# Splitting the first seven weight pieces on Pool, with a mask word spread over their shift

## The chip, the cores and the metric

The kernel runs on one core of one Trainium2 chip. Its five engines work side by side, each in the order of its own queue: TensorE (PE; its weight loads are listed apart as PEld), VectorE (DVE), ScalarE (ACT), GpSimd (Pool) and SyncE (SP), which here only issues DMAs. The metric is the device time of one execution in microseconds. Before the change it is 633.34 us, the median of three runs (632.31 to 634.42).

## The reference, cut to what matters

Attention with a local window and a few global keys, over 4 batches, 8 heads, 768 positions and a head size of 64, and then a feed-forward network (FFN) on the 3072 tokens that come out:

```
scores = q @ k^T / 8 + bias            # bias = -slope[head] * distance
scores = where(global | local, scores, -1e9)
x = softmax(scores) @ v                # 3072 tokens x 512
h = x @ w_in                           # 512 x 2048, float64
out = maximum(0.01 * h, h) @ w_out     # 2048 x 512, float64, result float32
```

`w_in` and `w_out` are float64 numbers. The kernel reads them as pairs of 32-bit words and turns every number into a sum of two rounded numbers (type fp32r), a high and a low part, so that three matmuls of fp32r stand for one exact product.

## The kernel before, in words

**The work and its stages.** The attention is cut into 48 units of one block of 128 queries and four heads. For a unit, TensorE makes the scores (L218), DVE adds the bias and finds the smallest value in one pass (L232), ACT takes exponentials with their sums (L245), DVE makes reciprocals (L266, L267), a diagonal matrix of them is made (`dg`, L284, by Pool in the first eight units and by DVE after), TensorE transposes and scales with it (L314), ACT copies the result (`pt`, L329), TensorE multiplies it by `v` (L360), and the product is split into a high part by ACT (`xh`, L387) and a low part by DVE (`xl`, L390).

The FFN takes the tokens in chunks: the first two of 384, the rest of 256. The weights lie in 32 pieces of 128 x 512 float64 (16 of `w_in`, 16 of `w_out`), and each is converted once. Seven of them (`LEAD_CONV`) are converted in the lead, which is the stage ahead of the FFN; the other 25 are converted between the FFN's first tiles.

**The lead.** The loop at the end of `fast_path` calls `lead_event(t)` for t = 0 to 7. Event t holds the scores of unit t, the product with `v` of unit t-2, the transposes of unit t-1, and from t = 1 on the conversion of piece t-1. The order of the instructions on every engine is written out by hand and pinned (`pin`, `keep_in_program_order`).

**A conversion** (`split_float64`) has six steps. `scale`: ACT turns the upper word into a float32 of the right exponent (L939). `shift`: DVE shifts its bits by three and masks them (L942), then brings the sign in from the upper word (L944). `low`: DVE brings in the upper bits of the lower word (L948). `high`: ACT rounds the number to its high part (L952). `rest`: DVE subtracts the high part from the number (L955). The work tile `w` of these steps has two buffers.

The first three steps of piece p stand in event p+1. Its last two, `high` and `rest`, are put on a list (`due`) and are issued in the event behind: `ends[0]()` at the event's beginning, `ends[1]()` behind the exponentials. So in event t the instructions of DVE stand in this order: four L232 of unit t, `rest` of piece t-2, both instructions of `shift` of piece t-1, the two small operations of `sums`, `low` of piece t-1, and L390 of unit t-2, which ends the event (in event 7, the last, `xl` stands behind the L232). Those of ACT: `high` of piece t-2, `scale` of piece t-1, four exponentials, the copy `pt` of unit t-1, `xh` of unit t-2. Pool has only `dg` of unit t, and, between units 0 and 1, eight small scalings of the bias table (L1010). The last two steps of the seventh piece (p = 6) stand in the FFN's first tile (j = 0).

**The loads.** SP issues the loads of q, k, v and of the weight pieces (L121), the latter three pieces ahead of their conversion, into four staging buffers. Two converted pieces of `w_in` are also written out to DRAM by SP early on (L886, `wd<-ring`), from a ring of two buffers that streams weights later.

Of the kernel before, what the change touches and what calls it, by code (L numbers as in the profile page):

```python
# [10 lines left out]
F32 = mybir.dt.float32  # L11
F32R = mybir.dt.float32r
BF16 = mybir.dt.bfloat16
I32 = mybir.dt.int32
I64 = mybir.dt.int64
AF = mybir.ActivationFunctionType
ALU = mybir.AluOpType
# [18 lines left out]
LEAD_CONV = 7  # L36
# [12 lines left out]
def copy_exact(eng, dst, src):  # L49
    return eng.tensor_scalar(out=dst, in0=src, scalar1=1.0, scalar2=1.0, op0=ALU.mult, op1=ALU.mult)  # L50
# [3 lines left out]
def fast_path(ctx, tc, qp, kp, vp, wi, wo, nvec, convert, nmall, out, B, H, S):  # L54
    nc = tc.nc
# [19 lines left out]
    raw = ctx.enter_context(tc.tile_pool(name="raw", bufs=2))  # L75
# [14 lines left out]
    stage = early.enter_context(tc.tile_pool(name="stage", bufs=STAGES, side="right"))  # L90
# [7 lines left out]
    small = const.tile([P, 32], F32, name="one")  # L98
    one, ones, fl = small[:, :1], small[:, 1:2], small[:, 4:8]
    flag = small[:1, 8:9].bitcast(I32)  # L100
    nc.vector.memset(one, 0.0)
    pinned_exp = nc.scalar.activation(out=one, in_=one, func=AF.Exp)
    tc.keep_in_program_order(pinned_exp)
# [3 lines left out]
    eye = const.tile([P, HALF], F32, name="eye")  # L107
    tc.keep_in_program_order(nc.vector.tensor_tensor(out=eye, in0=ident[:, :HALF], in1=ident[:, HALF:], op=ALU.add))
    convert()
    nbw = const.tile([P, H, KW], BF16, name="nbw")  # L110
    nb0 = const.tile([P, H, KW - HALF], BF16, name="nb0")

# [2 lines left out]
    staged = {}  # L115

    def load_piece(p):
        if p < len(pieces):
            m, f = pieces[p]
            t = stage.tile([P, NK * P], I64, tag="stage", name="wst", bufs=STAGES)  # L120
            pin(nc.sync.dma_start(out=t, in_=(wi, wo)[m][f].rearrange("p a b -> p (a b)")))  # L121
            staged[p] = t
# [10 lines left out]
    def conversion(p):  # L133

        m, f = pieces[p]
        to = wout[:, f] if m else win[f]
        dh, dl = to[:, 0], to[:, 1]
        if p:
            load_piece(p + STAGES - 2)
        scale, shift, low, *parts = split_float64(tc, pin, stage, staged.pop(p), dh, dl)  # L140
        due.extend(parts)
        return scale, shift, low

# [2 lines left out]
    LEAD = NU * CHUNKS[0]  # L146
# [234 lines left out]
    def parts(u, av):  # L381
        del units[u]
        av = av[:, :, 2 * KW:]
        xh, xl = slab(u)

        def high():
            pin(nc.scalar.copy(out=xh, in_=av))  # L387

        def low():
            pin(nc.vector.tensor_tensor(out=xl, in0=av, in1=xh.bitcast(F32), op=ALU.subtract))  # L390
        return high, low
# [12 lines left out]
    def lead_event(t, conv=(), between=lambda: None):  # L404

        av = (ps_lead if t % 2 else ps_x).tile([P, 2, 512], F32, tag="ps_av", name="ps_sc")
        high, low = [lambda: None] * 2
        last = t == LEAD + 1
        scores(t, av)
        if t > 1:  # L410
            ov = ps_lead.tile([P, 2, 512], F32, tag="ps_ov", name="ps_ov")
            attn_v(t - 2, ov)
            high, low = parts(t - 2, ov)
        if t:
            transposes(t - 1)
        if t:
            load_qk(t + 2)
        load_v(t)
        if t < 2:
            load_piece(t + 1)  # L420
        ends = due[:] or [lambda: None] * 2
        due.clear()
        ends[0]()
        if last:
            high()
        scale, shift, low_bits = conversion(conv[0]) if conv else [lambda: None] * 3
        scale()
        biased(t, av)
        if last:
            low()  # L430
        exps(t)
        between()
        ends[1]()
        shift()
        sums(t)
        low_bits()
        if t:
            keep_pt(t - 1)
        if not last:
            high()  # L440
            low()
# [315 lines left out]
    load_qk(2)  # L757
    warm(5)
    tabs = kept_rows.tile([P, 2, KW], BF16, name="tabs")
    tables = build_bias(tc, ffn, nb0, nvec, tabs, H)  # L760
    with tc.tile_pool(name="ps_l", bufs=1, space=bass.MemoryType.PSUM) as ps_lead:
        for t in range(LEAD + 2):
            lead_event(t, [t - LEAD - 2 + LEAD_CONV] if t >= LEAD + 2 - LEAD_CONV else (), *([] if t else [tables]))
            if t == 0:
                scale_bias(tc, tabs[:, 1], nbw, H, 1)
    ps_h = ctx.enter_context(tc.tile_pool(name="ps_h", bufs=1, space=bass.MemoryType.PSUM))
# [2 lines left out]
    for j in range(len(order)):  # L769
# [5 lines left out]
        scale, shift, low_bits = conversion(todo[0]) if todo else [lambda: None] * 3  # L775
# [5 lines left out]
        if events and j < LEFT:  # L781
            t = events[0]
# [11 lines left out]
            high, low = parts(t - 2, av)  # L794
# [78 lines left out]
        if j in twice:  # L873
            ends = due[:]
            due.clear()
            scale, shift, low_bits = conversion(todo[1])
# [47 lines left out]
    return last_pairs()  # L924


def split_float64(tc, pin, pool, raw, dh, dl):

    nc = tc.nc
    w2 = raw.bitcast(I32).rearrange("p (n two) -> p n two", two=2)
    lo, hi = w2[:, :, 0], w2[:, :, 1]
    w = pool.tile([P, lo.shape[1]], F32, tag="work", name="w32", bufs=2)
    wb = w.bitcast(I32)
    w3 = w.rearrange("p (a b) -> p a b", a=dh.shape[1]) if len(dh.shape) == 3 else w

    def scale():
        pin(nc.scalar.activation(out=w, in_=hi.bitcast(F32), func=AF.Copy, scale=2.0 ** -112))  # L939

    def shift():
        pin(nc.vector.tensor_scalar(out=wb, in0=wb, scalar1=3, scalar2=0x7FFFFFF8,  # L942
                                    op0=ALU.logical_shift_left, op1=ALU.bitwise_and))
        pin(nc.vector.scalar_tensor_tensor(out=wb, in0=hi, scalar=-0x80000000, in1=wb,  # L944
                                           op0=ALU.bitwise_and, op1=ALU.bitwise_or))

    def low():
        pin(nc.vector.scalar_tensor_tensor(out=wb, in0=lo, scalar=29, in1=wb,  # L948
                                           op0=ALU.logical_shift_right, op1=ALU.bitwise_or))

    def high():
        pin(nc.scalar.copy(out=dh, in_=w3))  # L952

    def rest():
        pin(nc.vector.tensor_tensor(out=dl, in0=w3, in1=dh.bitcast(F32), op=ALU.subtract))  # L955

    return scale, shift, low, high, rest


def build_bias(tc, work, nb0, nvec, tabs, H):  # L960

    nc = tc.nc
    pin = tc.keep_in_program_order
    loc = work.tile([P, 2 * P], F32, tag="gh", name="loc")
    far = work.tile([P, 2 * P], F32, tag="gl", name="far")
    col = work.tile([P, HALF], F32, tag="gh", name="col")
    n8 = work.tile([P, 1], F32, tag="gl", name="n8")
    first, tab = tabs[:, 0], tabs[:, 1]  # L970
    ng, nl = nvec[:, 0:1], nvec[:, 1:2]
    lo, hi = slice(0, HALF), slice(HALF, P)


    nc.gpsimd.iota(loc, pattern=[[8, 2 * P]], base=-8 * P, channel_multiplier=-8, allow_small_or_imprecise_dtypes=True)
    nc.gpsimd.affine_select(out=loc[:, P:], in_=loc[:, P:], pattern=[[-1, P]], compare_op=ALU.is_ge, fill=-BIG, base=0,
                            channel_multiplier=1)
    nc.gpsimd.iota(col, pattern=[[1, HALF]], base=0, channel_multiplier=0, allow_small_or_imprecise_dtypes=True)
    nc.gpsimd.memset(first[lo, HALF:P], -BIG)
    pin(nc.vector.tensor_scalar(out=n8, in0=nl, scalar1=-8.0, scalar2=None, op0=ALU.mult))  # L980
    pin(nc.vector.tensor_scalar(out=col, in0=col, scalar1=ng, scalar2=-BIG, op0=ALU.is_ge, op1=ALU.mult))
    pin(nc.vector.tensor_scalar(out=far, in0=loc, scalar1=n8, scalar2=-BIG, op0=ALU.is_le, op1=ALU.mult))
    pin(nc.vector.tensor_tensor(out=loc, in0=loc, in1=far, op=ALU.add))

    for part, x in ((lo, HALF), (hi, 0)):
        pin(nc.vector.scalar_tensor_tensor(out=first[part, HALF + x:P + x], in0=col[part], scalar=n8[part],
                                           in1=loc[part, P:P + HALF], op0=ALU.add, op1=ALU.max))
    pin(nc.vector.tensor_copy(out=first[hi, P:], in_=loc[hi, P + HALF:]))
    for h in range(H):
        pin(nc_scale(nc, nc.vector if h < H // NU else nc.scalar, nb0, first[:, HALF:], h, H, 1))  # L990

    def tables():
        for part, x, y in ((lo, HALF, G), (hi, 0, P - G)):
            pin(nc.vector.tensor_scalar(out=tab[part, x:x + G], in0=col[part, :G], scalar1=n8[part], scalar2=None, op0=ALU.add))
        pin(nc.scalar.copy(out=tab[lo, :HALF], in_=loc[lo, P - WIN:P - G]))
        pin(nc.scalar.copy(out=tab[lo, HALF + G:], in_=loc[lo, P - G:P + HALF]))
        pin(nc.scalar.copy(out=tab[hi, G:], in_=loc[hi, P - G:]))
    return tables
# [248 lines left out]
```

## Time and profile before

| What | Value |
|---|---|
| Time, median of three runs | 633.34 us |
| The profiled execution's own time | 633.62 us |
| Its span, from the first to the last instruction | 631.8 us |
| Mean clock granted to TensorE | 0.997 |
| Busy in 0 to 40 us: PE, DVE, ACT, Pool | 26.72, 33.59, 32.28, 11.71 us |
| Busy in 40 to 60 us: PE, DVE, ACT, Pool | 18.99, 18.31, 16.22, 3.53 us |
| Busy in 60 to 100 us: PE, DVE, ACT, Pool | 40.00, 33.91, 25.24, 3.30 us |
| DMA: share of time busy, 0 to 40 us | 0.84 |

How to read the profile. A row of the timeline gives the start and the duration in us, the engine, the line of the kernel, the operation, the tile written and the tiles read with their shapes, how many instructions the row stands for, and in brackets how long the engine stood idle before it and what ended that. Durations of two neighbours on one engine may overlap by some hundredths, because an instruction starts while the one ahead of it drains; so the time that an instruction takes on its engine is read from start to start. A row of a single line gives the count, the shortest, the median and the longest duration in ns, the first and the last start, and the shapes. The slices of the page cut the span into 40 equal parts; each digit is the busy share in tenths. The spans of Pool are rougher than those of the other engines.

### The profile page before, as it was taken

Reading aid. Unit: us, or ns where it says so; the run is one execution under the profiler, and the core shown is the slowest. Engines: PE = TensorE matmul, PEld = TensorE weight load, DVE = VectorE, ACT = ScalarE, POOL = GpSimd, SP = SyncE. Lnnn points to the kernel's source line nnn. Section 1 sums busy time; section 2 is a strip of 40 time slices with the busy share of each in tenths; the row PEclk is TensorE's granted clock in tenths of the full one; section 3 lists DMA queues with packets and bytes.
Section 4 is the critical chain, followed back from the end, with each engine's and each line's share of the span. In section 5 each row is a group of like instructions: output and inputs, shape, how many; then the busy total and the mean of one; then the engine's idle time right before and its main releaser. Section 6 shows DMA issues by size and latency. Waiting matters only on the chain.

```text
span 631.8 us, 16777 instructions
## 1 busy us (share of the span) xinstructions
PE 609.2 (96%) x6546; PEld 561.9 (89%) x6546; DVE 457.7 (72%) x1308; ACT 345.3 (55%) x901; POOL 68.6 (11%) x118
## 2 busy tenths in 40 slices
PE   5789999999999999999999999999999999999994
PEld 4578899988888888899999999999999999999994
DVE  7988879995566996966986765765765766754653
ACT  6987755554435556546556555545655655522321
POOL 4212200000101001011012101101101100110000
PEclk9999999999999999999999999999999999999998
DMA  7886645633547755765765865855865864633321
GB/s 262 312 307 196 198 146 188 200 109 122 159 140 243 243 186 183 227 206 192 227 219 175 264 239 162 262 175 172 247 229 182 258 211 143 217 102 101 134 68 38
DMA packets 63336, 120.72 MB, mean 191 GB/s; under 512 B 8976, under 2 KB 28432, under 8 KB 63248
## 3 DMA queue, kind: packets, MB, share of 16 engines
q1 hardware_dynamic: 52880, 82.34, 40.5%
q10 hardware_dynamic: 10368, 37.23, 18.0%
q8 instruction: 53, 0.87, 0.6%
q14 instruction: 35, 0.29, 0.2%
HBM read 96.21 MB, written 23.33 MB: 189 GB/s over the span
## 4 chain that ended last, share of the span: by engine, by line
PE 85%; DVE 6%; DMA 4%; ACT 3%; issue 1%; SPq 0%; DVEq 0%; ACTq 0%
PE ps_m L612 21%; PE ps_p L556 16%; PE ps_h L556 15%; PE ps_h L472 9%; PE ps_q L612 7%; PE ps_av L360 5%; PE ps_av L218 3%; PE ps_o L1180 3%; PE ps_o L1179 3%; PE ps_o L1181 3%; ACT pr L245 2%; DMA ring<-wd 1%; DVE pr L232 1%; DMA via<-pr 1%; DVE w L948 1%
## 5 line engine op out<-in xcount | busy, mean ns | idle before, releaser
L578 ACT CAST gh<-t 128x896 fp32r<-128x896 f32 (+1 forms) x73 | 62.2, 853 | 100.0 <-DVE t L572 57.5
L581 DVE TENSOR_TENSOR gl<-t,gh 128x896 fp32r<-128x896 f32 (+1 forms) x73 | 71.1, 974 | 47.9 <-ACT gh L578 47.9
L245 ACT ACTIVATE pr<-pr,nmall 128x192 f32<-128x192 f32 (+1 forms) x192 | 83.3, 435 | 25.4 <-DVE nmall L232 25.4
L612 PE MATMUL ps_m<-wout,gh 128*128 128x256 f32 (+1 forms) x396 | 85.9, 299 | 0.0
L569 DVE SCALAR_TENSOR_TENSOR t<-t 128x512 f32<-128x512 f32 x72 | 49.6, 689 | 33.0 <-ACT t L567 31.8
L50 POOL TENSOR_SCALAR xh<-x 128x256 fp32r<-128x256 f32 x36 | 22.7, 631 | 433.1 <-ACT x L366 352.6
L472 PE MATMUL ps_h<-xh,win 128*128 128x384 f32 x224 | 62.7, 341 | 0.2 <-DVE xl L390 0.2
L612 PEld LDWEIGHTS ps_m<-wout,gh 128*128 128x128 f32 x396 | 61.4, 188 | 1.6
L612 PE MATMUL ps_m<-wout,gl 128*128 128x256 f32 (+1 forms) x198 | 59.2, 299 | 0.0
L556 PE MATMUL ps_p<-xh,win 128*128 128x256 f32 x288 | 58.3, 287 | 0.0
L556 PE MATMUL ps_h<-xh,win 128*128 128x256 f32 x288 | 56.8, 282 | 0.0
L556 PE MATMUL ps_h<-xh,ring 128*128 128x256 f32 x288 | 55.6, 278 | 0.0
L556 PE MATMUL ps_p<-xh,ring 128*128 128x256 f32 x288 | 55.3, 277 | 0.4 <-DMA ring<-wd 0.4
L572 DVE TENSOR_TENSOR t<-t 128x128 f32<-128x128 f32 x216 | 53.1, 284 | 2.8
L556 PEld LDWEIGHTS ps_p<-xh,win 128*128 128x128 f32 x288 | 46.3, 188 | 6.0 <-issue 5.0
L556 PEld LDWEIGHTS ps_h<-xh,win 128*128 128x128 f32 x288 | 46.5, 188 | 2.4 <-issue 2.2
L232 DVE CUSTOM_DVE_ANT_0 pr<-ps_av,nbw 128x192 f32<-128x192 f32 x136 | 40.3, 351 | 11.1 <-ACT x L366 9.3
L612 PE MATMUL ps_m<-h,gh 128*128 128x256 f32 (+1 forms) x162 | 46.9, 290 | 0.0
L556 PEld LDWEIGHTS ps_p<-xh,ring 128*128 128x128 f32 x288 | 46.2, 188 | 0.6 <-DMA ring<-wd 0.6
L556 PEld LDWEIGHTS ps_h<-xh,ring 128*128 128x128 f32 x288 | 46.4, 189 | 0.0
L612 PE MATMUL ps_m<-h,gl 128*128 128x256 f32 x162 | 45.0, 278 | 0.0
L612 PE MATMUL ps_m<-l,gh 128*128 128x256 f32 x162 | 45.0, 278 | 0.0
(154 smaller groups left out, 1567.1 us busy)
## 6 DMA issues: line engine op xcount, KB each, us to landing
ring<-wd ACTq DMA_DIRECT2D x70, 512.0 KB, 3.6
via<-pr SPq DMA_DIRECT2D x30, 384.0 KB, 3.2
pt_d<-via SPq DMA_DIRECT2D x120, 96.0 KB, 3.2
vr<-in_vp_dram SPq DMA_DIRECT2D x40, 256.0 KB, 3.4
kr<-in_kp_dram SPq DMA_DIRECT2D x39, 256.0 KB, 4.0
wst<-in_wi_dram SPq DMA_DIRECT2D x16, 512.0 KB, 4.5
wst<-in_wo_dram SPq DMA_DIRECT2D x16, 512.0 KB, 4.5
qs<-in_qp_dram SPq DMA_DIRECT2D x24, 256.0 KB, 4.5
```

The lines of the kernel that those rows point to most:

```text
L50: return eng.tensor_scalar(out=dst, in0=src, scalar1=1.0, scalar2=1.0, op0=ALU.mult, op1=ALU.mult)
L218: tc.keep_in_program_order(nc.tensor.matmul(own(u, av[qf, j, a * KW:(a + 1) * KW]), lhsT=q[rows, a, qf], rhs=keys(rows, a, f), start=True, ...
L232: pin(nc.vector.tensor_tensor_reduce(out=head(u, pr, a, j), in0=own(u, ps[:, j, a * KW:(a + 1) * KW]), in1=nb, scale=-0.125, scalar=3.0e38 ...
L245: pin(nc.scalar.activation(out=p, in_=p, func=AF.Exp, scale=-1.0, bias=nm[:, 2 * a + j:2 * a + j + 1], accum_out=sm[:, 2 * a + j:2 * a + j ...
L360: tc.keep_in_program_order(nc.tensor.matmul(av[out, a, cols], lhsT=v[rows, t, j, :], rhs=near(rows, j, t, fs), start=(n == 0), stop=(n == ...
L472: tc.keep_in_program_order(nc.tensor.matmul(ps, lhsT=win[f][:, y, k], rhs=xt[c][x][:, k, :ct], start=(k + i == 0), stop=(k == NK - 1 and i ...
L556: tc.keep_in_program_order(nc.tensor.matmul(o, lhsT=w[:, y, k], rhs=x[:, k, :], start=(k + i == 0), stop=(k == NK - 1 and i == 2)))
L569: pin(nc.vector.scalar_tensor_tensor(out=g, in0=g, scalar=0.01, in1=g, op0=ALU.mult, op1=ALU.max))
L572: pin(nc.vector.tensor_tensor(out=t[:, o], in0=t[:, x], in1=t[:, y], op=op))
L578: pin(nc.scalar.copy(out=gh[:, i - a0:j - a0], in_=t[:, i:j]))
L581: pin(nc.vector.tensor_tensor(out=gl[:, i - a0:j - a0], in0=t[:, i:j], in1=gh[:, i - a0:j - a0].bitcast(F32), op=ALU.subtract))
L612: tc.keep_in_program_order(nc.tensor.matmul(to, lhsT=x[:, a], rhs=y, start=first and n == 0, stop=last and n == 2))
```

## The change

For the seven pieces of the lead (`p < LEAD_CONV`), `high` and `rest` go to Pool: the rounding as a multiplication by one (`copy_exact`, an existing helper), the subtraction as before. Their places in the order of the program stay. Of the shift, the shift with its mask becomes an operation on two tensors, by DVE as before: the mask is no longer a constant of the instruction but a word in a column of `small`, spread over the 512 elements. This word is made in two steps: a memset of the column, and in event 0, behind the exponentials, an operation on that column. The other 25 pieces are converted as before.

```
+    mask = small[:, 10:11].bitcast(I32)
...
+    make_mask = lambda: pin(nc.vector.tensor_scalar(out=mask, in0=mask, scalar1=0, scalar2=0x7FFFFFF8,
+                                                    op0=ALU.bitwise_and, op1=ALU.bitwise_or))
...
-        scale, shift, low, *parts = split_float64(tc, pin, stage, staged.pop(p), dh, dl)
+        scale, shift, low, *parts = split_float64(tc, pin, stage, staged.pop(p), dh, dl, mask if p < LEAD_CONV else None)
...
+    nc.vector.memset(small[:, 10:11], 0.0)
...
-            lead_event(t, [t - LEAD - 2 + LEAD_CONV] if t >= LEAD + 2 - LEAD_CONV else (), *([] if t else [tables]))
+            lead_event(t, [t - LEAD - 2 + LEAD_CONV] if t >= LEAD + 2 - LEAD_CONV else (), *([] if t else [lambda: (tables(), make_mask())]))
...
     def shift():
-        pin(nc.vector.tensor_scalar(out=wb, in0=wb, scalar1=3, scalar2=0x7FFFFFF8,
-                                    op0=ALU.logical_shift_left, op1=ALU.bitwise_and))
+        if mask is None:
+            pin(nc.vector.tensor_scalar(out=wb, in0=wb, scalar1=3, scalar2=0x7FFFFFF8,
+                                        op0=ALU.logical_shift_left, op1=ALU.bitwise_and))
+        else:
+            pin(nc.vector.scalar_tensor_tensor(out=wb, in0=wb, scalar=3, in1=mask.to_broadcast(list(wb.shape)),
+                                               op0=ALU.logical_shift_left, op1=ALU.bitwise_and))
         pin(nc.vector.scalar_tensor_tensor(out=wb, in0=hi, scalar=-0x80000000, in1=wb,
                                            op0=ALU.bitwise_and, op1=ALU.bitwise_or))
...
     def high():
-        pin(nc.scalar.copy(out=dh, in_=w3))
+        pin(copy_exact(nc.gpsimd, dh, w3) if mask is not None else nc.scalar.copy(out=dh, in_=w3))

     def rest():
-        pin(nc.vector.tensor_tensor(out=dl, in0=w3, in1=dh.bitcast(F32), op=ALU.subtract))
+        eng = nc.gpsimd if mask is not None else nc.vector
+        pin(eng.tensor_tensor(out=dl, in0=w3, in1=dh.bitcast(F32), op=ALU.subtract))
```

More of the change, by code (lines that the diff above doesn't have):

```diff
@@ L924, in fast_path, with split_float64 @@
     return last_pairs()
-def split_float64(tc, pin, pool, raw, dh, dl):
+def split_float64(tc, pin, pool, raw, dh, dl, mask=None):
     nc = tc.nc
```

## The prediction, made before the change was run

> **What bounds the kernel now.** I read the page first (busy shares, the span in 40 slices), then the timeline of the first 45 us, since the seven pieces are converted there, then single lines of Pool and windows in which Pool and DVE work at once.
>
> ```profile
> span 631.8 us, 16777 instructions
> ...
> PE 609.2 (96%) x6546; PEld 561.9 (89%) x6546; DVE 457.7 (72%) x1308; ACT 345.3 (55%) x901; POOL 68.6 (11%) x118
> ...
> PE   5789999999999999999999999999999999999994
> ...
> DVE  7988879995566996966986765765765766754653
> ACT  6987755554435556546556555545655655522321
> ```
>
> Over the span TensorE is the bound. Only in the first slices (15.8 us each) is it not, and there DVE and ACT are nearly full. Behind them TensorE has next to no idle time in which a delay of the lead could vanish: what the lead gains or loses, the end gains or loses. One event of the lead, in the timeline (start, duration, engine, line):
>
> ```profile
> 16.77 0.42 DVE L390 TENSOR_TENSOR xl<-ps_ov,xh 128x256 fp32r<-128x256 f32 x1
> ...
> 24.89 0.42 DVE L390 TENSOR_TENSOR xl<-ps_ov,xh 128x256 fp32r<-128x256 f32 x1
> ...
> 25.22 0.34 DVE L232 CUSTOM_DVE_ANT_0 pr<-ps_sc,nbw 128x192 f32<-128x192 f32 x1
> ...
> 26.33 0.68 DVE L955 TENSOR_TENSOR wout<-w,wout 128x512 fp32r<-128x512 f32 x1
> ...
> 26.93 0.42 DVE L942 TENSOR_SCALAR w<-w 128x512 int32<-128x512 int32 x1
> ...
> 27.39 0.69 DVE L944 SCALAR_TENSOR_TENSOR w<-wst,w 128x512 int32<-128x512 int32 x1
> ...
> 28.07 0.17 DVE L266 TENSOR_SCALAR rs<-sm 128x4 f32<-128x4 f32 x1
> 28.27 0.18 DVE L267 RECIPROCAL rs<-rs 128x4 f32<-128x4 f32 x1
> 28.37 0.66 DVE L948 SCALAR_TENSOR_TENSOR w<-wst,w 128x512 int32<-128x512 int32 x1
> ...
> 28.62 0.88 POOL L284 TENSOR_TENSOR dg<-eye,rs 128x256 f32<-128x256 f32 x1 [3.18 <-DVE rs L267]
> 28.95 0.42 DVE L390 TENSOR_TENSOR xl<-ps_ov,xh 128x256 fp32r<-128x256 f32 x1
> 29.06 0.62 ACT L952 CAST win<-w 128x512 fp32r<-128x512 f32 x1
> ...
> 29.59 0.69 ACT L939 ACTIVATE w<-wst 128x512 f32<-128x512 f32 x1
> ...
> 33.01 0.42 DVE L390 TENSOR_TENSOR xl<-ps_ov,xh 128x256 fp32r<-128x256 f32 x1
> ```
>
> From one L390 to the next is 4.06 us, and DVE goes through it without a gap. By starts: L390 0.33, four L232 1.11, the subtraction L955 0.60, the shift L942 0.46, the or L944 0.68, sums 0.20 and 0.10, low bits L948 0.58. Four such periods (events 3 to 6) lie between 16.77 and 33.01. Pool does one thing in a period, the dg product.
>
> **What leaves.** ACT loses L952, 0.53 to its next start (29.06 to 29.59), DVE loses L955, 0.60. Both stand in the full part of the lead, so this is the gain on offer.
>
> **The shift.** As an operation on two tensors it has L944's form, 0.69 for the same 512 elements, instead of 0.42. The or needs its result and starts 0.04 behind its end today (26.93 + 0.42 = 27.35, start 27.39), so 0.46 becomes 0.73. The word of the mask costs a memset of one column and one 128x1 operation, both in the first event or ahead of it, where DVE stands idle for ACT:
>
> ```profile
> 8.73 0.17 DVE L266 TENSOR_SCALAR rs<-sm 128x4 f32<-128x4 f32 x1 [0.80 <-ACT pr L245]
> ```
>
> The 0.80 hides an operation of 0.17; uncovered it would cost that, once.
>
> **Event 2**, the first with a subtraction, supplies the or's price without a wait, and a first look at what Pool does to DVE:
>
> ```profile
> 13.76 0.61 POOL L284 TENSOR_TENSOR dg<-eye,rs 128x256 f32<-128x256 f32 x1
> ...
> 13.88 1.05 DVE L955 TENSOR_TENSOR win<-w,win 128x512 fp32r<-128x512 f32 x1
> ...
> 14.85 0.41 DVE L942 TENSOR_SCALAR w<-w 128x512 int32<-128x512 int32 x1
> ...
> 15.30 0.69 DVE L944 SCALAR_TENSOR_TENSOR w<-wst,w 128x512 int32<-128x512 int32 x1
> ...
> 15.91 0.16 DVE L266 TENSOR_SCALAR rs<-sm 128x4 f32<-128x4 f32 x1
> ...
> 16.20 0.66 DVE L948 SCALAR_TENSOR_TENSOR w<-wst,w 128x512 int32<-128x512 int32 x1
> ```
>
> Here the or takes 0.61 (15.30 to 15.91). Undisturbed, the period would thus be 4.06 - 0.60 + 0.27 - 0.07 = 3.66: 0.40 saved.
>
> **What Pool takes.** No Pool row has 512 elements. The nearest (min/median/max ns, then two rows of the timeline):
>
> ```profile
> L1010 POOL TENSOR_SCALAR nbw<-tabs x16: 350/351/779, 9.8 to 59.3; 128x192 bf16<-128x192 bf16 x16
> L1010 POOL TENSOR_SCALAR nb<-tabs x8: 297/324/787, 64.0 to 71.7; 128x128 bf16<-128x128 bf16 x8
> ```
>
> ```profile
> 152.66 0.40 POOL L50 TENSOR_SCALAR xh<-x 128x256 fp32r<-128x256 f32 x1 [80.53 <-ACT pr L245]
> 153.15 0.74 POOL L397 TENSOR_TENSOR xl<-x,xh 128x256 fp32r<-128x256 f32 x1
> ```
>
> With one input 297, 350 and about 400 ns at 128, 192 and 256 elements are 0.83 ns an element on 0.19 us, so the high part is 0.19 + 0.43 = 0.62 (bounds 0.40, one row of half its size, and 0.80, two). The subtraction has two inputs: 0.74 at 256, of which 0.19 fixed, gives 0.19 + 2 x 0.55 = 1.29 at 512. Its bounds are 0.95 (second half at the one-input slope) and 1.48 (twice 0.74); I take 1.29, as its fixed part is read from three sizes. A dependent Pool instruction starts 0.09 behind (153.06 to 153.15). [...]
>
> **Pool and DVE hold each other up.** Beside dg (13.76 to 14.37) L955 took 1.05 instead of 0.68: it ended at 14.93 as if begun at 14.25, 0.12 ahead of dg's end. The reverse: dg at 28.62 took 0.88 instead of 0.61, as if begun at 28.89, when L948 was nearly through. Later, with the same operation as the one that moves:
>
> ```profile
> 224.23 0.79 POOL L397 TENSOR_TENSOR xl<-x,xh 128x256 fp32r<-128x256 f32 x1
> ...
> 224.34 0.96 DVE L592 TENSOR_TENSOR wk<-wout 128x256 f32<-128x256 f32 x1
> ```
>
> ```profile
> L592 DVE TENSOR_TENSOR wk<-wk,wout 128x256 f32<-128x256 f32 x42 | 17.3, 424 | 0.2
> ```
>
> 0.96 instead of 0.42: as if begun at 224.88, 0.14 ahead of Pool's end at 225.02. So a DVE instruction with two inputs in SBUF waits for a Pool instruction that was there first, less 0.13. L390 and L232, with one input in PSUM, don't: L390 at 28.95 has its 0.42 beside dg. [...]
>
> Now the steady event, counted from L390's start. Dg ends at 0.55 (29.50 against 28.95). The high part, queued behind it, 0.55 to 1.17; subtraction 1.26 to 2.55. DVE is through L232 at 1.44 and wants the shift, with two inputs in SBUF: it is let in at 2.42, a wait of 0.98. Behind it queue the or, the sums (and so dg) and the low bits, the whole rest of the event. Period 3.66 + 0.98 = 4.64, that is 0.58 more than 4.06; over four periods +2.3.
>
> Event 2: the shift wants to start at 13.88, gets in behind dg at 14.25; the high part, waiting since 14.37, comes next (14.78 to 15.40) and holds the or to 15.27; the subtraction gets in behind the or, about 15.80 to 17.09; the low bits start at 16.96 instead of 16.20: +0.75.
>
> **Events 7 and after.** The last subtractions fall here:
>
> ```profile
> 37.24 0.17 DVE L266 TENSOR_SCALAR rs<-sm 128x4 f32<-128x4 f32 x1 [0.31 <-ACT pr L245]
> ...
> 42.14 0.42 DVE L390 TENSOR_TENSOR xl<-ps_av,xh 128x256 fp32r<-128x256 f32 x1
> ...
> 42.66 0.90 PE L360 MATMUL ps_av<-pt,vr 64*64 64x128 f32 x32 [0.26 <-ACT pr L245]
> ```
>
> In event 7 the sums wait for ACT's exponentials, so a held shift costs nothing. In the first FFN tile the chain goes L390, then L360, which overwrites the bank that L390 reads; without the seventh L955 ahead of it, DVE comes sooner, and up to TensorE's wait of 0.26 is won. I book all of it: TensorE is full behind it, so no more can be.
>
> **Queues.** SP sends ring weights to DRAM when their subtraction is done, with loads behind it:
>
> ```profile
> 22.98 0.33 SPq L886 DMA_DIRECT2D wd<-ring  x1
> ...
> 23.84 0.74 SPq L121 DMA_DIRECT2D wst<-in_wo_dram  x1
> ```
>
> ```profile
> wst<-in_wo_dram SPq DMA_DIRECT2D x4, 512.0 KB, 5.3
> ```
>
> That piece lands at 29.14, its scale L939 starts at 29.59: 0.45 to spare. Pool ends this subtraction 2.55 into its event, where DVE ended it at 22.96, 2.1 after its own event began, so the load comes 0.4 later within the event; but the events are longer, and it stays in time. ACT, 0.53 shorter, is not late. The converted pieces themselves are wanted microseconds later.
>
> **The sum.** 2.3 + 0.75 - 0.26 = +2.8. The profiled execution took 633.62 us (span 631.8), 0.3 above the median of 633.34; I add to the median: 636.1. With the subtraction at 0.95 or 1.48, five events change by 0.34 or 0.19 each: +1.1 or +3.7. A measurement of this kernel tells about 0.3% (1.9 us) from no change.
>
> **Rivals.** (1) Faster: the shift by two tensors isn't held, because a spread word is read differently from a full tensor, which no row shows. Then events 3 to 6 give 4 x 0.40, event 2 gives 0.68 (no L955 with its 0.37 of waiting), the first tile 0.26: -2.5, 630.8. Against it: L944, L948 and L955 are of this kind, and are held or hold. (2) The same, but the loads become late: with periods of 3.66 event 6 wants its piece near 27.0, and SP can't issue it before the ring's subtraction is done (19.75 + 2.55, near 22.4) and 0.9 more, landing at 28.6: 1.5 of the gain go, -1.0, 632.3, no measurable change. (3) Slower still: Pool comes a little later (from a high part beyond 0.8, say), so that the shift slips in ahead of the subtraction, or ahead of the high part when that is not begun by 1.44; then the or is held for the high part too, 0.48 more in each of four periods: +4.7, 638.0. It decides at 1.44 in the event.
>
> **How the numbers follow.** Holding as worked out 0.72, of which 0.12 within 0.3% (a subtraction nearer 0.95); rival 1 0.12; rival 2 0.10; rival 3 0.06. Hence slower 0.66, same 0.22, faster 0.12. The range runs from 632.8 to 638.1: it takes in both bounds of the subtraction (634.4, 637.0), a share of rival 2 and rival 3, and leaves rival 1 out.
>
> **What would show it.** Right: Pool rows of about 0.62 and 1.29 per piece; L390 to L390 near 4.6; the shift's row near 1.7, its own 0.69 plus the wait; the L390 that is at 33.01 now near 36. Wrong: shift rows of 0.69 beside a running Pool subtraction (rival 1), L939 waiting for a load (rival 2), long rows of both shift and or in every event (rival 3), or a period of 4.6 with an unchanged end, if TensorE could make up the lead's delay.

## The result, and the profile after

The changed kernel takes 635.58 us (median of 7 runs, 635.24 to 640.07); the kernel before, on the same chip between them, 632.51 us (7 runs, 632.02 to 634.42). The ratio is 1.0056, with a 95% interval of 1.0039 to 1.0073: slower, by about 3.1 us. The profiled execution took 635.27 us.

From the page of the changed kernel, the lines that answer to those of before (the last is the clock granted to TensorE, in tenths):

```profile
span 633.5 us, 16779 instructions
...
PE 611.1 (96%) x6546; PEld 564.3 (89%) x6546; DVE 459.7 (73%) x1303; ACT 341.8 (54%) x894; POOL 83.7 (13%) x132
...
PE   5689999999999999999999999999999999999996
...
DVE  7989879996565997875987765765765765744654
ACT  6778755555344655555555654654664564522321
...
PEclk9789999999999999999999999999999999999999
```

ACT is 3.5 us less busy, Pool 15.1 us more, and DVE, which lost seven subtractions, is 2.0 us more busy. A row's duration includes the time in which the instruction is held (the shift's rows below: 0.69 and 1.60), so DVE's gain sits inside longer rows. One event of the lead shows where. Timeline of the changed kernel; line numbers grow by 3 up to L393 and by 4 to 9 behind it (the shift is L950, the or L952, the low bits L956; Pool's high part is L50 and its subtraction L964):

```profile
26.25 0.90 POOL L287 TENSOR_TENSOR dg<-eye,rs 128x256 f32<-128x256 f32 x1 [1.71 <-DVE rs L270]
26.60 0.41 DVE L393 TENSOR_TENSOR xl<-ps_ov,xh 128x256 fp32r<-128x256 f32 x1
...
27.13 0.61 POOL L50 TENSOR_SCALAR wout<-w 128x512 fp32r<-128x512 f32 x1
...
27.82 1.27 POOL L964 TENSOR_TENSOR wout<-w,wout 128x512 fp32r<-128x512 f32 x1
...
28.04 1.60 DVE L950 SCALAR_TENSOR_TENSOR w<-w,one 128x512 int32<-128x512 int32 x1
29.68 0.69 DVE L952 SCALAR_TENSOR_TENSOR w<-wst,w 128x512 int32<-128x512 int32 x1
30.29 0.16 DVE L269 TENSOR_SCALAR rs<-sm 128x4 f32<-128x4 f32 x1
...
30.58 0.66 DVE L956 SCALAR_TENSOR_TENSOR w<-wst,w 128x512 int32<-128x512 int32 x1
...
31.16 0.42 DVE L393 TENSOR_TENSOR xl<-ps_ov,xh 128x256 fp32r<-128x256 f32 x1
...
35.72 0.42 DVE L393 TENSOR_TENSOR xl<-ps_ov,xh 128x256 fp32r<-128x256 f32 x1
...
38.15 0.69 DVE L950 SCALAR_TENSOR_TENSOR w<-w,one 128x512 int32<-128x512 int32 x1 [0.16 <-ACT w L943]
```

From L393 to L393 is 4.56 us, where it was 4.06. The shift takes 0.69 where Pool's subtraction is all but done (38.15; it ends at 38.23) and 1.60 where it has just begun. It ends at 29.64, as if begun at 28.95; Pool's subtraction ends at 29.09. So DVE is let in 0.14 ahead of Pool's end, having waited 0.91. Everything behind the shift comes later by that. The xl of event 6, at 33.01 before, is at 35.72: 2.71 later, of which 0.61 is lost in event 2 and the rest in the four periods.

Event 2 takes another path than the steady events. Changed kernel, then the kernel before:

```profile
9.79 4.82 POOL L1019 TENSOR_SCALAR nbw<-tabs 128x192 bf16<-128x192 bf16 x8
...
14.58 1.04 POOL L287 TENSOR_TENSOR dg<-eye,rs 128x256 f32<-128x256 f32 x1
...
15.67 0.69 PE L317 MATMUL ps_tr<-dg,pr 64*64 64x64 f32 x32 [2.65 <-POOL dg L287]
...
17.38 0.42 DVE L393 TENSOR_TENSOR xl<-ps_ov,xh 128x256 fp32r<-128x256 f32 x1 [0.64 <-ACT xh L390]
```

```profile
9.78 4.02 POOL L1010 TENSOR_SCALAR nbw<-tabs 128x192 bf16<-128x192 bf16 x8
...
14.43 1.13 PE L314 MATMUL ps_tr<-dg,pr 64*64 64x64 f32 x32 [1.42 <-POOL dg L284]
```

Here DVE holds Pool: the spread shift stretches Pool's eight scalings from 4.02 to 4.82 (the or beside them takes 0.71 in both kernels, and with the constant shift below the scalings stay at 4.02). The dg product behind them is late and itself held (1.04 instead of 0.61), and the transposes wait for it. The chain transposes, pt, xh, xl ends the event, with DVE waiting 0.64 for xh.

Then there is a loss on TensorE itself. TensorE in the first FFN tile, changed kernel, then before:

```profile
38.64 0.52 PE L475 MATMUL ps_h<-xl,win 128*128 128x384 f32 x1
...
41.53 0.90 PE L363 MATMUL ps_av<-pt,vr 64*64 64x128 f32 x32
...
46.00 0.90 PE L363 MATMUL ps_av<-pt,vr 64*64 64x128 f32 x32
```

```profile
35.62 0.33 PE L472 MATMUL ps_h<-xl,win 128*128 128x384 f32 x1
...
37.87 0.90 PE L360 MATMUL ps_av<-pt,vr 64*64 64x128 f32 x32 [0.19 <-ACT pt L329]
```

The same matmul takes 0.52 instead of 0.33. At the end of this tile the product with v starts 3.66 later than before: 0.95 on top of the 2.71. One tile on, 46.00 stands against 42.66, 3.34 later: the 0.26 of waiting that stood there is gone. That matmuls ran slow is the granted clock (windows; the columns are busy time of each engine with the count, then clock, DMA share and GB/s), in the changed kernel:

```profile
10.00:20.00 10.00, 6.71 (x180) 5.37 (x184) 9.01 (x29) 7.45 (x29) 9.52 (x14) 0.83 0.70 249
20.00:30.00 10.00, 5.97 (x200) 5.12 (x196) 9.86 (x29) 7.08 (x24) 6.24 (x7) 0.84 0.75 255
30.00:40.00 10.00, 6.94 (x198) 6.03 (x191) 9.05 (x31) 7.32 (x24) 5.55 (x6) 0.84 0.97 327
```

Before, all three windows have 1.00; the last of them, and two rows of TensorE in the kernel before:

```profile
30.00:40.00 10.00, 7.86 (x272) 6.97 (x264) 8.52 (x29) 8.72 (x27) 1.76 (x2) 1.00 0.91 320
```

```profile
19.22 1.50 PE L218 MATMUL ps_sc<-kr,qs 64*64 64x192 f32 x16
...
22.72 0.83 PE L218 MATMUL ps_sc<-kr,qs 64*64 64x192 f32 x16
```

The column does not show a slow start: the same sixteen matmuls take 1.50 and then 0.83, and the clock reads 1.00 for both. Until the matmuls have once reached the shorter time (near 20 us here, near 26 in the run with the constant shift below) their rows are the better witness. In event 2 of the changed kernel TensorE had already left this slow start (32 transposes in 0.69, against 1.13 in the kernel before; both rows stand above).

Behind the first tiles the delay stays: SP's load of a flag late in the kernel comes at 617.4 instead of 613.8, 3.6 later. The stretch behind it differs from execution to execution (18.0 us in the profiled run of before, 16.1 in that of after; 16.2 and 17.7 in the second profiles of both), which is why the two spans differ by only 1.7.

### The profile page after: what moved, and what is told of

Same layout as the page of the kernel before. It is cut to its first block, busy times and chain, and to the rows that moved or that the text cites. A ratio compares the mean times of both kernels' runs of the same rounds, so it can differ in the third digit from the quotient of the medians.

```text
span 633.5 us, 16779 instructions
## 1 busy us (share of the span) xinstructions
PE 611.1 (96%) x6546; PEld 564.3 (89%) x6546; DVE 459.7 (73%) x1303; ACT 341.8 (54%) x894; POOL 83.7 (13%) x132
## 3 DMA queue, kind: packets, MB, share of 16 engines
q1 hardware_dynamic: 52880, 82.34, 40.6%
## 4 chain that ended last, share of the span: by engine, by line
PE 83%; DVE 7%; ACT 3%; DMA 3%; issue 1%; POOL 1%; SPq 0%; DVEq 0%; ACTq 0%
PE ps_m L615 21%; PE ps_p L559 15%; PE ps_h L559 14%; PE ps_h L475 10%; PE ps_q L615 6%; PE ps_av L363 4%; PE ps_av L221 3%; PE ps_o L1189 3%; PE ps_o L1188 3%; PE ps_o L1190 3%; ACT pr L248 2%; DMA ring<-wd 1%; PE ps_tr L317 1%; DVE w L950 1%; DVE pr L235 1%
## 5 line engine op out<-in xcount | busy, mean ns | idle before, releaser
L50 POOL TENSOR_SCALAR xh<-x 128x256 fp32r<-128x256 f32 x36 | 22.6, 628 | 433.7 <-ACT x L369 353.1
```

## The experiments

The theory (HOLD): a DVE instruction whose inputs all lie in SBUF waits for the Pool instruction that reads SBUF and was there first, whatever the shift's form. The rivals: the spread mask word is the cost; any Pool instruction holds DVE, one that only writes too; the low clock makes the events long; the loads come late. Each experiment changes the changed kernel as its diff says. Times are medians, with the ratio to the kernel before on the same chip and its interval. The median of before was 632.37 beside the constant shift, the mask alone, the high part alone and the dummies, 632.59 beside the subtraction alone, the two memset runs and the five high parts, and 633.12 beside the last four.

**The change with the constant shift.** Pool keeps both parts; the shift is again the one-input operation with a constant.

```
-        if mask is None:
+        if True:
```

> The change with its shift back as an operation on one tensor and a constant; both parts of the split stay on Pool. Theory HOLD (a DVE instruction with two inputs in SBUF, or the constant shift, waits until Pool's subtraction is done, and this wait lengthens each event): the constant shift is held just like the spread one, its row near 1.35 us instead of 1.61 (0.42 plus the same 0.92 of waiting), the period from one L393 to the next 4.56 - 0.27 = 4.29, the total about 1.4 us below the changed kernel and 1.5 above the one before. Rival FORM (the slower form of the shift is the cost and Pool's work is harmless): period near 3.4, total at or below the kernel before. [...]

635.29 us, 1.0038 (1.0022 to 1.0055). Its timeline:

```profile
23.04 1.27 POOL L964 TENSOR_TENSOR ring<-w,ring 128x512 fp32r<-128x512 f32 x1
23.26 1.34 DVE L947 TENSOR_SCALAR w<-w 128x512 int32<-128x512 int32 x1
...
32.70 0.49 DVE L947 TENSOR_SCALAR w<-w 128x512 int32<-128x512 int32 x1 [0.77 <-ACT w L943]
```

The one-input shift is held too: 1.34 instead of 0.42, let in 0.13 ahead of Pool's end. The period of event 3 is 4.30, as HOLD has it; events 4 and 5 take 4.53 and 4.06, as xl waits for xh there once (0.16, at 26.35) and the next shift then meets less of the subtraction (1.10). Pool's rows are those of the changed kernel (0.61 and 1.27): the constant shift holds Pool no longer than the spread one here. Event 2 goes as the prediction had it for the changed kernel: the scalings stay at 4.02, dg holds the shift (0.78), Pool's two new rows hold the or (0.98) and L269 (1.23), the low bits start at 16.94, and the event loses 0.75. The time is higher than expected: the period of event 6 is 4.99, since the shift waited 0.77 for a late load (32.70; more below), and the clock fell to 0.66 between 30 and 40 us.

**The mask alone.** Both parts go back to ACT and DVE; the shift stays on two tensors.

```
-        pin(copy_exact(nc.gpsimd, dh, w3) if mask is not None else nc.scalar.copy(out=dh, in_=w3))
+        pin(nc.scalar.copy(out=dh, in_=w3))
...
-        eng = nc.gpsimd if mask is not None else nc.vector
+        eng = nc.vector
```

> The spread mask alone: both parts of the split back on ACT and DVE. HOLD: nothing on Pool but dg, all shift rows at 0.69; the DVE period is 4.06 + 0.27 less the 0.07 for which DVE waits for ACT, 4.26; over events 1 to 6 about 1.2 us above the kernel before, clearly below the changed kernel. FORM: the whole loss comes back, about 3 us above before. Rival CLOCK (TensorE's lower granted clock in the lead, 0.84 against 1.00, makes the lead longer, whatever Pool does): no statement about the period, but the clock tells whether longer events alone lower it: if so, below 1.00 in 20 to 40 us here too.

634.67 us, 1.0029 (1.0013 to 1.0045). A shift of a steady event:

```profile
24.23 0.68 DVE L950 SCALAR_TENSOR_TENSOR w<-w,one 128x512 int32<-128x512 int32 x1
```

From event 4 on the period is 4.24 (4.36 in event 3): the mask costs 0.18 a period there, and the spread word is read at the price of a full tensor (0.68, beside 0.69 of the or). Event 2 loses 1.05 by the path shown above, so the mask alone, through Pool's scalings, makes that loss. The time is 2.3 above before, nearer FORM's 3 than HOLD's 1.2. HOLD's sum had neither event 2's loss nor the clock in it, and the clock is 0.66 between 30 and 40 us here too, with nothing of the conversion on Pool. The trace tells the two apart in the steady events: 4.24 here and 4.56 in the changed kernel, so the mask is not the whole loss. But either half of the change brings most of the 3.1 us by itself (the mask 2.3, Pool's part with the constant shift 2.9), and the two do not add up.

**The high part alone on Pool**, constant shift, subtraction on DVE.

> Only the high part on Pool; subtraction on DVE and constant shift as before. HOLD: Pool is done with the high part at about 1.17 of the event, DVE wants its subtraction at 1.44, so no row is held; period 4.06 less the 0.07 of waiting for ACT, 3.99; total 0 to 0.5 us below the kernel before. If each instruction on Pool cost in proportion to its length wherever it stands (rival SHARE): 0.61 of 1.89, about 1 us above before.

633.04 us, 1.0014 (0.9999 to 1.0029). The period is 3.98, 0.08 less than before; but the first high part stands behind the scalings and dg on Pool, and event 2 loses 0.74, more than the four periods bring. The total, 0.7 above, can't tell HOLD (0 to 0.5 below) from SHARE (about 1 above); the period can, and the run with five high parts below takes event 2 out.

**The subtraction alone on Pool**, high part on ACT, constant shift.

> Only the subtraction on Pool; high part on ACT and constant shift as before. HOLD: ACT ends the high part at 0.7 of the event, Pool's subtraction runs from 0.8 to 2.1, so the shift, wanted at 1.44, is let in near 1.93: its row 0.42 + 0.5 = 0.9. DVE then needs 3.39 + 0.5 = 3.9, below the 4.06 of the way low bits, high part, scale, exponentials, sums over ACT, which is unchanged: period 4.06, the held row costs nothing, total within 1 us of the kernel before, 2 us or more below the changed one. If Pool's subtraction cost by its length wherever it starts (SHARE): 1.28 of 1.89 of the loss, about 2 us above before.

634.71 us, 1.0028 (1.0011 to 1.0044), 2.1 above before, where HOLD had at most 1 and SHARE about 2. The total is SHARE's; the periods are not. In the timeline the shift comes when the subtraction is half done, and waits for what is left of it:

```profile
21.93 1.29 POOL L964 TENSOR_TENSOR ring<-w,ring 128x512 fp32r<-128x512 f32 x1 [0.26 <-ACT ring L960]
22.63 0.87 DVE L947 TENSOR_SCALAR w<-w 128x512 int32<-128x512 int32 x1
```

Periods are 4.04, 3.99 and 4.00, none longer than the 4.06 of before, and then 4.75, as ACT waited 0.67 for a load there. Event 2 loses 0.37. The hold scales with the overlap, as HOLD says. To the xl of event 6 all that makes 0.9. In event 7 TensorE then stands for 1.23 ahead of its last transpose on nothing that the profile names (it says "issue"), and the next product with v is 1.83 late (39.70). Whether the edit brings that stand is open.

**Dummy matmuls against the low clock.** The whole change, with six matmuls behind the scores of events 2 to 7 whose result is read by nobody.

```
+            for _ in range(6):
+                tc.keep_in_program_order(nc.tensor.matmul(av[:, 0, 2 * KW:], lhsT=ident, rhs=ident, start=True, stop=True))
```

> The changed kernel with six extra matmuls of 128 x 128 behind the scores in events 2 to 7, into unused columns, where TensorE waits for L393; their result is read by nobody. They keep TensorE busy in the lead. HOLD: the granted clock in 10 to 40 us goes from 0.84 to near 1.00, the period stays at 4.56 (DVE and Pool set it), and only the first FFN tile's matmuls in event 7 get shorter (0.52 to 0.34 each): 0.5 to 0.9 us below the changed kernel. CLOCK: the period falls back to about 4.1 and the total to the kernel before. If the extra matmuls stand in the way, above the changed kernel with TensorE late for L363.

638.56 us, 1.0089 (1.0068 to 1.0110), 3 above the changed kernel where 0.5 to 0.9 below was expected. A window of it, and a shift (line numbers are 2 higher here):

```profile
20.00:30.00 10.00, 8.11 (x254) 7.11 (x247) 9.86 (x31) 7.66 (x27) 6.42 (x7) 1.00 0.71 237
```

```profile
24.65 1.61 DVE L952 SCALAR_TENSOR_TENSOR w<-w,one 128x512 int32<-128x512 int32 x1
```

The clock reads 1.00 throughout the lead, yet the period is still 4.56 and the shift's row 1.61: the clock is not what makes the events long. What it costs shows in the first FFN tile: from the lead's last L393 to the next product with v are 3.03 here and 3.97 in the changed kernel, 0.94. The dummies delay event 2 by 1.26 themselves, and the profiled run stands 0.3 behind that of the changed kernel at 200 us and 1.2 behind near 618 us. Its span is 3.2 longer; the other 2.0 lie in the last 18 us. These 2.0 and the 0.9 between 200 and 618 us stay unexplained.

**Pool writes, but doesn't read.** The whole change, but instead of its subtraction Pool runs three memsets of the same tile, a little longer together. The low parts of the seven pieces are then zero, here, in the next run and in the first of the last four.

```
+        if mask is not None:
+            for _ in range(3):
+                pin(nc.gpsimd.memset(dl.bitcast(F32), 0.0))
+            return
```

> The changed kernel, but Pool's subtraction for the seven pieces is replaced by three memsets of the low part, so these low parts are zero: Pool works about as long on the same tile, but reads nothing from SBUF. The high part still is Pool's. HOLD in its wide form (any Pool instruction holds a DVE instruction with two inputs): shift rows of 1.2 or more, period above 4.1. [...] FORM: unchanged against the changed kernel.

634.37 us, 1.0023 (1.0007 to 1.0040). Its timeline:

```profile
22.64 1.69 POOL L966 MEMSET ring<- 128x512 f32 x3
...
23.16 0.69 DVE L950 SCALAR_TENSOR_TENSOR w<-w,one 128x512 int32<-128x512 int32 x1
...
24.36 0.33 SPq L890 DMA_DIRECT2D wd<-ring  x1
...
29.18 0.88 PE L221 MATMUL ps_sc<-kr,qs 64*64 64x192 f32 x16 [1.75 <-DMA kr<-in_kp_dram]
...
32.30 0.68 ACT L943 ACTIVATE w<-wst 128x512 f32<-128x512 f32 x1 [3.32 <-DMA wst<-in_wo_dram]
```

Beside 1.69 of memsets the shift takes 0.69: it isn't held. Nor does it slip in between two memsets at their cost: they take 1.68 in event 6 too, where the shift comes later. So what holds the shift is that Pool reads: 1.60 beside the subtraction, 0.69 beside the memsets. Undisturbed, a period is 3.65 (events 4 and 5). But the gain doesn't arrive: event 2 loses 1.03, by the mask's path, and event 6 lasts 6.69, because ACT waited 3.32 for its weight piece and TensorE 1.75 for its keys.

**The same with the constant shift.**

> As the kernel with memsets in place of Pool's subtraction (the low parts of the seven pieces are zero), but with the constant shift on one tensor. [...] If the constant shift is not held by writes: rows of 0.42, period 3.5, set by ACT (scale, exponentials, pt, xh). In both cases the total is within 0.5 us of the kernel with memsets and the spread mask; a clearly larger one would say that the spread mask serves to let Pool write.

633.51 us, 1.0012 (0.9994 to 1.0029). Events 4 and 5 take 3.67 and 3.66 (the shift is shorter by 0.24 from start to start, the or and L269 longer by as much), event 6 takes 7.34, with waits of 4.06 (ACT, the piece) and 2.25 (TensorE, keys) for loads.

**High parts of pieces 1 to 5 alone on Pool**, constant shift, to have the third run's period without its loss in event 2.

> The high parts of pieces 1 to 5 alone on Pool (those of the first and the last piece on ACT again), subtraction on DVE, constant shift. HOLD: event 2 and the first FFN tile as in the kernel before, since no high part queues behind the bias table's scalings or behind dg there; four periods of 3.98; the L393 that stood at 33.01 at about 32.7, the total 0.3 us below the kernel before, less than the measurement can tell. SHARE: above before.

632.69 us, 0.9988 (0.9973 to 1.0003). The period is 3.98, event 2 loses nothing, and event 6's xl is at 32.69, 0.32 sooner than before; the end can't be told from before. SHARE had it above. It is the best complete version here. Its clock was 0.83, 1.00 and 0.86 in the three windows, though events 2 to 6 are no longer than before. In event 7 TensorE stands for 2.03 ahead of its last transpose, again at "issue", where the kernel before has no such stand; and its first dip (16.6 to 20.0) falls where the kernel before is still in its slow start.

**The loads set free.** What held the loads above? The guess was SP's queue: the write of ring weights (L890) waits for Pool's result, and the next loads stand behind it. In these two runs that write is pinned to its place in the FFN loop, far behind (issued at 40.15 and 42.79); the first has the memsets and the constant shift, the second the whole change with the constant shift.

```
-            nc.sync.dma_start(out=wd[f // 2], in_=win[f].rearrange("p a k x -> p (a k x)").bitcast(F32))
+            wr = nc.sync.dma_start(out=wd[f // 2], in_=win[f].rearrange("p a k x -> p (a k x)").bitcast(F32))
+            if f == 1:
+                tc.keep_in_program_order(wr)
```

> As the run with memsets and the constant shift (the low parts of the seven pieces stay zero), but the first write of the ring to DRAM is issued much later, so that nothing stands ahead of the loads in SP's queue while Pool works. Loads held by that write: the scale of event 6 (L943) starts without its wait of 1.85 us, TensorE's scores without theirs of 2.25, all periods stay near 3.66, and the xl of event 6 starts near 31.5 us instead of 35.2; the end comes 1 to 3 us sooner than the 633.51 of that run, 630.5 to 632.5, the upper end if the clock is low again in the first FFN tile. Loads held by the bandwidth of the DMA engines (the rival): the waits shrink by less than half, xl of event 6 not before 34, and the time stays at 633 to 633.5.

630.24 us, 0.9953 (0.9936 to 0.9969). Its timeline, with one wait for a load left between 10 and 40 us, in event 5:

```profile
24.62 0.42 DVE L393 TENSOR_TENSOR xl<-ps_ov,xh 128x256 fp32r<-128x256 f32 x1
25.02 0.71 ACT L945 ACTIVATE w<-wst 128x512 f32<-128x512 f32 x1 [0.53 <-DMA wst<-in_wi_dram]
...
28.46 0.42 DVE L393 TENSOR_TENSOR xl<-ps_ov,xh 128x256 fp32r<-128x256 f32 x1
...
30.36 0.83 PE L221 MATMUL ps_sc<-kr,qs 64*64 64x192 f32 x16
...
32.11 0.42 DVE L393 TENSOR_TENSOR xl<-ps_ov,xh 128x256 fp32r<-128x256 f32 x1
```

Event 6 falls from 7.34 to 3.65 and ends at 32.11 (31.5 was expected: event 2 ended 0.6 later). Event 5 takes 3.84. DMA share is 0.97 between 20 and 30 us, and still no load of event 6 is late: it was the queue, not the bandwidth. The clock reads 1.00 in the whole lead. It is 0.5% faster than before, but it leaves out the low parts.

> As the run of the whole change with the constant shift, but the first write of the ring to DRAM is issued much later. If the late load cost that run its last period: the fifth period falls from 5.00 to 4.3 or 4.5, no wait of L943 in event 6, and the time from 635.3 to about 634.6. If the period was long for another reason (the clock), it stays near 5.0 and the time near 635.3.

634.56 us, 1.0028 (1.0012 to 1.0045), as expected: the period of event 6 is 4.30 instead of 4.99, and the shift waits for no load there. The interval overlaps that of the constant shift above, so the gain is shown by the trace and not by the times.

**Both kernels once more**, unchanged, one execution each.

> The kernel before, unchanged, profiled once more. If the lower granted clock in the lead belongs to the change, this shows 1.00 from 10 to 40 us and its first FFN tile's matmuls at 0.34 us, ps_av's first L360 near 37.9. If the clock falls by chance from run to run, it can be near 0.8 here too.

> The changed kernel, unchanged, profiled once more. If the lower clock belongs to the change: again 0.8 to 0.85 in the lead and near 0.95 us lost in the first FFN tile. If it falls by chance: 1.00 is possible, and then ps_av's first L363 starts near 40.6 instead of 41.53; the periods are 4.56 either way.

631.91 and 636.96 us. Before: 1.00 in all three windows, L360 at 37.86, the flag at 613.9. After, the window of 30 to 40 us:

```profile
30.00:40.00 10.00, 6.56 (x178) 5.71 (x179) 8.73 (x30) 5.71 (x19) 5.53 (x6) 0.66 0.84 295
```

Its periods are 4.64, 4.57, 4.56 and 4.56, L363 at 41.98, the flag at 617.5: 3.6 later than before again. From event 6's xl to L363 are 5.74, against 5.81 in the first profile and 4.86 in the kernel before, so the clock cost 0.88 here. The low clock came back with the change, at other places. Over the timed runs, the mean clock's median is 0.996 for before, 0.991 to 0.994 for the seven experiments in which an event or a load of the lead takes longer, and 0.997 to 0.998 for the dummies, the five high parts and the free loads with memsets. So the loss goes with a longer lead, but not strictly: the five high parts dipped in their profile with events 2 to 6 no longer, and the subtraction alone did not dip.

Finer windows of the same traces show what a dip is. In the changed kernel the clock stands at 0.50 from 16.7 to 20.1, from 26.9 to 30.3 and from 37.2 to 40.6, 3.41 us each time, and the starts lie 10.24 apart, three times 3.41. In all eight profiles with a dip between 10 and 45 us the dips last 3.41 or twice that. Cut each of them into windows of 3.41 that end where its dips begin: in the window ahead of a dip TensorE was busy for 26 to 44% (30, 37 and 34% in the changed kernel), and windows at full clock with 47% or more were not followed by one; both the 26% and the 47% come from the memsets with the constant shift. As an estimate from the waits in the rows of TensorE, a period of 4.06 with 1.8 of waiting leaves TensorE at least 1.6 of any 3.41, which is 47%; one of 4.56 with 2.3 of waiting can leave 1.1, 33%. The dummies, which fill part of the wait, have no dip (1.00 in all three windows). In the second profile of the changed kernel the dips stand elsewhere: the three windows of 10 us have 1.00, 0.83 and 0.66, where the first profile has 0.83, 0.84 and 0.84. So how many dips there are and what they hit differs between two executions of one kernel; what makes the clock fall is not shown.

## Why the prediction was right

**What leaves and the undisturbed period.** Predicted 3.66; two periods of the memset run with the spread shift have 3.65. Right. ACT's and DVE's shorter lists were worth 0.40 a period, and came only with memsets in place of Pool's subtraction. (The two memset runs with the constant shift have 3.65 to 3.67 too, but by another sum: a shorter shift, a longer or and L269.)

**Pool's rows.** 0.62 and 1.29 predicted, 0.61 and 1.27 to 1.28 measured (1.58 to 1.59 where they had to wait for DVE in turn). The straight lines from smaller sizes carried to 512 elements.

**The hold.** Wait 0.98 predicted, 0.91 measured; the row near 1.7 is 1.60; the period 4.64 is 4.56. DVE does get in 0.14 ahead of Pool's end, as the rows of before had it.

**Event 2.** Predicted +0.75, measured +0.61, by a path that the prediction didn't have. It followed Pool's new work holding the low bits; the first harm is DVE's longer shift holding Pool's scalings and dg (the mask alone lost 1.05 there). The size was near by luck, twice over: the first profile had its transposes at full speed already. In the second they were slow, as in the kernel before:

```profile
15.77 1.13 PE L317 MATMUL ps_tr<-dg,pr 64*64 64x64 f32 x32 [2.65 <-POOL dg L287]
```

There they took 1.13 instead of 0.69, and the event lost 1.14 to the same point; the mask alone and the memsets with the mask, also with 1.13, lost 1.05 and 1.03. The predicted path is real, but of the runs here only those with the constant shift and both parts on Pool take it.

**Events 7 and after.** The held shift doesn't fall there (0.69 at 38.15), and the wait of 0.26 is gone, as forecast. The reason given, the seventh subtraction off DVE, fits the runs at full clock (from one product with v to the next 4.46 with the dummies and 4.47 with the free loads, 4.79 before), but a slow first tile does it alone: 4.47 with the mask alone and 4.46 with five high parts, whose seventh subtraction stays on DVE. In the changed kernel the two can't be told apart. Not foreseen: 0.95 lost to the clock in the first tile. The prediction named no cost for TensorE waiting longer.

**The queue of SP.** Predicted: the piece issued 0.4 later within its event, and in time. In the changed kernel:

```profile
24.57 0.33 SPq L890 DMA_DIRECT2D wd<-ring  x1
25.00 0.38 SPq L189 DMA_DIRECT2D kr<-in_kp_dram  x1
...
26.25 0.45 SPq L124 DMA_DIRECT2D wst<-in_wo_dram  x1
```

The issue is 2.41 later than before (23.84), also because the write now stands ahead of a load of keys that went first before (20.78, L186). ACT then waited 0.41 for the piece (31.52), but the shift wanted it at 32.60 and had it at 32.24. In time, by a third of a microsecond. In the second profile ACT waited 1.79 for the same piece, until 32.45, and the shift had its input at 33.15, wanted at 33.12: no margin left, and in shorter events the piece is late.

**The sum.** Predicted +2.8. By the trace: four periods 2.10, event 2 0.61, clock 0.95, first tile back 0.32: +3.34, which is the 46.00 against 42.66; by the medians +3.07. The periods were over-sized by 0.2 and event 2 by 0.14, and the missing clock, 0.95, was larger than both. That 635.58 lies 0.5 below 636.1 comes from the base, 632.51 instead of 633.34; the change itself cost 0.3 more than forecast. So the wait, which makes the sum, was right in kind and nearly in size; that the total came so near is in part luck, as a missing term and three that were off by less stand against each other, and event 2 can lose 0.5 more.

**The rivals.** Not held (rival 1): refuted by the shift's 1.60. Loads late (rival 2): not the changed kernel's fate, since its events are long, but a real bound on what could be won: 3.68 in one event with memsets, where the prediction had 1.5. The or held too (rival 3): seen once, in event 3, where the shift slipped in ahead of the subtraction (0.74) and the or took 1.65 instead; that period was 4.66.

## What to carry to other kernels

Before work goes to Pool to relieve DVE, lay its reads beside DVE's next instruction with all its inputs in SBUF (those with one in PSUM, like L393 beside dg, kept their 0.42): here the relief was paid back as far as the two overlapped (0.91 of waiting a period), while memsets left the two-input shift its 0.69. Then follow the moved result into the DMA queues, since the write that waited for it here held the loads behind it (4.06 and 2.25 of waiting with the memsets and the constant shift); moving one write took the ratio from 1.0012 to 0.9953. And where TensorE waits longer, look at the granted clock ahead of the next full stage, in windows of a few us: a mean of 0.84 over 10 us was a clock of 0.50 for a third of them.

## What the hardware showed beyond expectation

The one-input DVE instructions on SBUF seen here (tensor_scalar) are held by a reading Pool instruction just as the two-input shift is (1.34 instead of 0.42, beside 1.60 instead of 0.69), even one of 4 elements: L269 took 0.57 instead of 0.16 beside dg in event 2. Beside memsets the two-input shift is free (0.69), but the one-input shift is not quite: three memsets took 1.84 to 1.85 beside it instead of 1.69, and L269 stayed until their end (0.33).
